# Gated linear attention and a rational MLP: the first super block half plain and half wide, the last one summed in natural order

## The chip, the core and the metric

The kernel runs on one core of one Trainium2 chip. The core has a matrix engine (TensorE, "PE" in the profile, with its weight loads shown apart as "PEld"), a vector engine (VectorE, "DVE"), a scalar engine (ScalarE, "ACT"), a general engine (GpSimd, "POOL") and a queue engine (SyncE, "SP") that here issues the DMA transfers. SBUF is the working memory of 128 partitions. PSUM is the memory of 8 banks into which TensorE writes its sums; one bank holds 512 float32 values in each partition.

The metric is the device time of one execution in microseconds. A run of a program gives one such time, and a profiled execution gives a trace beside it.

## The reference

```python
def _attn_ref(q, k, v, alpha):              # (4, 8, 768, 48) each
    state = zeros((B, H, D, D))
    for t in range(S):
        state = alpha[:, :, t, :, None] * state + einsum('bhd,bhe->bhde', k[:, :, t], v[:, :, t])
        y[:, :, t] = einsum('bhd,bhde->bhe', q[:, :, t], state)

def _moe_ref(x, w_in, w_out, a, b):         # x (3072, 384), w_in (384, 2048), w_out (2048, 384)
    h = x @ w_in
    P = a[0] + a[1]*h + a[2]*h**2 + a[3]*h**3
    Q = 1.0 + abs(b[0])*abs(h) + abs(b[1])*h**2
    return (P / (Q + 1e-06)) @ w_out
```

A gated linear attention over 4 batches of 768 tokens and 8 heads gives x with 384 columns; a two-layer MLP with a rational function between the layers follows. The weights arrive as float64, the rest as float32.

## The kernel before

**Attention.** The tokens are worked in 24 groups g of 128. For each group the kernel loads alpha, k and q (`load_akq`, four parts each, or `load_nat` for the first four groups), turns them so that channels lie on partitions (`turn_x`, L425, on VectorE, one transpose each for a, k and q; for the first four groups transposes on TensorE, L398, and copies, L417), takes running products of the gates (`suffix` L428, `prefix` L440, both scans on VectorE), scales k and q with them (L455, L458), multiplies scores (`sc_mm`, L472), masks them and adds up the output and the new state (`attn_mm`, L514 and L533). The scans read a small constant, the floor, from PSUM: groups below `G3` = 8 from bank 3, later ones from a cell in bank 5 that is written anew each time (`set_floor`, L344). The output of a group goes from PSUM to x (`x_hi` L556, `x_lo` L561).

**Weights.** `w_in` and `w_out` are loaded as 64-bit words in 16 blocks, ("i", j) and ("o", j) for j = 0 to 7 (`load_w`, L239 and L242). Each is made into float32 by integer steps: a scaled copy of the high word (`join_abs`, ScalarE, L249), a shift of the low word (`join_low`, VectorE, L255), the sign (`join_sign`, ScalarE L259 or VectorE L261) and the joining (`join`, VectorE, L274), which writes into the word buffer. For the wide jobs a block is brought back into a work buffer by a DMA (`bring`, L282) and split into a high and a low part (`split_hi` ScalarE L289, `split_lo` L294).

**MLP.** It is done in 96 jobs u. A job covers 512 values of h in each partition. The first 512 tokens (two segments of 256) take 16 "plain" jobs: float32 matmuls of unsplit weights, one block j (256 rows of h) and one segment at a time (`mlp_in` L589, `mlp_out_hi` L699). Their outputs lie in natural order, tokens on partitions, and are summed in banks 6 and 7 in two phases (`PHASES` = 0 and 6): first blocks 0 to 5 of both segments, then blocks 6 and 7, added onto the first part (`mlp_done`, L726 and L728) and stored (L731). The other 2560 tokens take 80 "wide" jobs, five super blocks m = 1 to 5 of 512 tokens with 16 jobs each, one for each 128 rows of h: nine float32r matmuls of split operands in (`wide_in`, L608), nine out (`wide_out`, L619), summed transposed, channels on partitions, in the three banks `O_BANKS` = 6, 7, 3. At the end of a super block VectorE turns the banks in 32x32 blocks into `parts` (`wide_done`, L625), and twelve scattered stores follow (`wide_store`, L629).

Between the two layers every job runs the rational function: ScalarE L635, L638, L644 (or GpSimd L642), L665, L668; GpSimd L647; VectorE L658, L662, L672, L675, L681. Wide jobs add the high part of the result (`act_gh`, ScalarE, L684) and the low part (`sub_gl`, GpSimd or now and then VectorE, L688).

**The end.** A check that all gates lie within limits (`guard`, `verdict_*`) gives one flag; all engines load it (L1049) and branch (L1050) past a general version of the kernel that isn't run with these inputs.

**The order.** All steps are registered with `add(key, engine, cost, function, arguments, what must come before, ..., alt=another engine)`. The order in which they are issued, and which engine takes a step with an alternative, is written out: the compressed list `ORDER` holds the number of each step, with a mark for the alternative. The costs and due times in `add` were for drawing up that list and have no effect when the kernel is built. Each engine works its own instructions strictly in this order.

Of the kernel before, what the change touches and what calls it, by code (L numbers as in the profile page):

```python
# [12 lines left out]
F32 = mybir.dt.float32  # L13
# [11 lines left out]
class Plan:  # L25
# [61 lines left out]
    'iiLEM!G^AxVZq1=s!@Cs<b-MI%3<!!JSYH~}S3M*mlpq@O8Cz;`V6#nB{yalH6QdkAkxfjpkFmA=mxHV7X$sxUm&fw*|',
# [35 lines left out]
    ';IEGteDD#2_aov5|GWtj1d)P7LE->{kN%TS7}x-V$iXKUC7^(VBtg_5X^<>P9z+Xb1Sx`)LChd}5GzO(qz=*qX@hh@`X',  # L123
    'EElCdd?I4l)L9gZ}}JD{Y|',
]


PACE, T0, LEAD = 5.0, 20.0, 2.0
NBI = 2
UPO = 16  # L130
NPH = 2
PHASES = (0, 6)
DMA = 0.49
SV = (1.1, 2.03, 0.67, 0.46)
IN = (1.09, 1.31)
OH = (0.722, 1.3)
WIDE = 0.229
G3 = 8
# [943 lines left out]
```

## Time and profile before

| | us |
|---|---|
| three runs | 549.97, 550.0, 548.46; median 549.97 |
| the profiled execution | 548.87, span of its trace 547.2 |
| TensorE busy | 522.2 (95%) |
| VectorE busy | 488.3 (89%) |
| ScalarE busy | 439.6 (80%) |
| GpSimd busy | 387.3 (71%) |
| DMA | 59.83 MB, mean 109 GB/s |
| granted TensorE clock | 0.991 of full |

The page of the profile gives busy time of each engine, a picture of the span in 40 slices, the chain of work that ended last, and the costliest groups of instructions by line, engine, output and input tile, with the number of instructions, busy time and mean duration of one, and the idle time before them. Matmuls overlap in the records, so the mean duration of one (397 ns in L608) is longer than their distance; the distance is read from the chain, where matmuls in a row are merged ("PE ps L608 x9"). A plain float32 matmul leaves two records, a float32r matmul one.

### The profile page before, as it was taken

What the parts mean: (1) busy time and instruction counts of PE and PEld (TensorE: products, weight loads), DVE (VectorE), ACT (ScalarE), POOL (GpSimd) and SP (SyncE); (2) the same over time, 40 slices, a digit from 0 to 9 for tenths busy, and PEclk for the clock granted to TensorE, in tenths of its full rate; (3) what the DMA queues carried; (4) which work ended last, traced back from release to release, by engine and by line L of the source; (5) the groups of instructions that cost most, each with busy time, mean ns of one, the idle gap of its engine ahead of it and who ended that gap; (6) DMA issues with size and microseconds to landing.
All of it is one profiled execution on the core that took longest, in us unless ns stands there. A gap on an engine that the chain in (4) does not pass through costs nothing.

```text
span 547.2 us, 11680 instructions
## 1 busy us (share of the span) xinstructions
PE 522.2 (95%) x4238; PEld 414.9 (76%) x4238; DVE 488.3 (89%) x753; ACT 439.6 (80%) x721; POOL 387.3 (71%) x358
## 2 busy tenths in 40 slices
PE   8879979999999999999999999999999999999990
PEld 8667657777778887788788787878888778878870
DVE  3999999999999998998999999999999897878871
ACT  3789869767889898888888978888878788889860
POOL 2557557778899898787877877867868576666750
PEclk9999999999999999999999999999999999999996
DMA  7898566556564543543366253523316120220003
GB/s 216 246 305 249 142 168 173 123 138 156 156 130 121 142 131 109 123 95 83 79 134 137 56 131 65 127 70 76 85 37 137 32 59 1 42 37 1 1 0 62
DMA packets 149343, 59.83 MB, mean 109 GB/s; under 512 B 133152, under 2 KB 141856, under 8 KB 149280
## 3 DMA queue, kind: packets, MB, share of 16 engines
q1 hardware_dynamic: 149280, 59.03, 43.6%
q8 instruction: 35, 0.57, 0.5%
q14 instruction: 28, 0.23, 0.1%
HBM read 47.98 MB, written 4.72 MB: 96 GB/s over the span
## 4 chain that ended last, share of the span: by engine, by line
PE 80%; DMA 6%; SPq 5%; DVE 4%; ACT 1%; issue 1%; DVEq 0%; ACTq 0%
PE ps L608 30%; PE ps L619 30%; PE ps L514 6%; PE ps L699 5%; PE ps L589 4%; PE ps L472 4%; DMA wo_words<-in_moe_w_out_dram 3%; DMA wi_words<-in_moe_w_in_dram 2%; SPq L374 2%; PE ps L490 1%; SPq L239 1%; PE ps L533 1%; SPq L381 1%; DMA raw_a<-in_alpha_dram 1%; SPq L210 1%
## 5 line engine op out<-in xcount | busy, mean ns | idle before, releaser
L608 PE MATMUL ps<-x,wi 128*128 128x512 f32 x720 | 195.0, 397 | 1.2 <-DVE t L681 1.2
L608 PEld LDWEIGHTS ps<-x,wi 128*128 128x128 f32 x720 | 133.9, 188 | 33.8 <-DVE t L681 2.4
L647 POOL TENSOR_TENSOR qm<-qm,ah 128x512 f32<-128x512 f32 x96 | 128.1, 1335 | 37.6 <-ACT qm L644 31.7
L619 PE MATMUL ps<-gh,wo 128*128 128x512 f32 x480 | 133.4, 398 | 0.0
L688 POOL TENSOR_TENSOR gl<-t,gh 128x512 fp32r<-128x512 f32 x70 | 91.0, 1302 | 39.1 <-ACT gh L684 19.4
L619 PEld LDWEIGHTS ps<-gh,wo 128*128 128x128 f32 x480 | 87.9, 188 | 20.4 <-ACT gh L684 0.3
L638 ACT ACTIVATE t<-ps,coef 128x512 f32<-128x512 f32 x96 | 74.1, 773 | 15.8 <-PE ps L608 9.3
L658 DVE TENSOR_TENSOR t<-t,ps 128x512 f32<-128x512 f32 x96 | 65.2, 679 | 19.1 <-ACT t L638 11.3
L665 ACT ACTIVATE ps<-qm,one_eps 128x512 f32<-128x512 f32 x96 | 66.3, 691 | 18.7 <-DVE t L662 12.4
L672 DVE SCALAR_TENSOR_TENSOR t<-t,coef,ps 128x512 f32<-128x512 f32 x96 | 70.7, 737 | 8.7 <-ACT ps L668 7.6
L635 ACT ACTIVATE ah<-ps 128x512 f32<-128x512 f32 x96 | 56.9, 592 | 25.1 <-PE ps L608 20.0
L662 DVE SCALAR_TENSOR_TENSOR t<-t,coef,ps 128x512 f32<-128x512 f32 x96 | 70.8, 738 | 1.3
L619 PE MATMUL ps<-gl,wo 128*128 128x512 f32 x240 | 69.1, 396 | 0.0
L681 DVE SCALAR_TENSOR_TENSOR t<-ps,t 128x512 f32<-128x512 f32 x96 | 65.8, 685 | 1.7
L675 DVE SCALAR_TENSOR_TENSOR ps<-qm,ps 128x512 f32<-128x512 f32 x96 | 65.9, 687 | 0.0
L642 POOL TENSOR_SCALAR qm<-ah,bab 128x512 f32<-128x512 f32 x44 | 37.8, 858 | 35.9 <-ACT ah L635 22.7
L668 ACT ACTIVATE ps<-ps 128x512 f32<-128x512 f32 x96 | 56.2, 586 | 1.8
L684 ACT ACTIVATE gh<-t 128x512 fp32r<-128x512 f32 x80 | 50.0, 625 | 5.1 <-DVE t L681 5.1
L619 PEld LDWEIGHTS ps<-gl,wo 128*128 128x128 f32 x240 | 44.3, 188 | 10.7 <-POOL gl L688 0.6
L589 PE MATMUL ps<-x,wi_words 128*128 128x256 f32 x192 | 47.3, 386 | 3.8 <-DVE t L681 3.4
L699 PE MATMUL ps<-wo_words,t 128*128 128x384 f32 x128 | 46.9, 490 | 0.0
L589 PEld LDWEIGHTS ps<-x,wi_words 128*128 128x128 f32 x192 | 35.3, 190 | 14.0 <-DVE t L681 4.5
(104 smaller groups left out, 748.2 us busy)
## 6 DMA issues: line engine op xcount, KB each, us to landing
raw_a<-in_alpha_dram SPq DMA_DIRECT2D x160, 48.0 KB, 2.1
raw_q<-in_q_dram SPq DMA_DIRECT2D x160, 48.0 KB, 2.1
raw_k<-in_k_dram SPq DMA_DIRECT2D x160, 48.0 KB, 2.1
wo_words<-in_moe_w_out_dram SPq DMA_DIRECT2D x8, 768.0 KB, 5.5
wi_words<-in_moe_w_in_dram SPq DMA_DIRECT2D x8, 768.0 KB, 6.7
tv<-in_v_dram SPq DMA_DIRECT2D x24, 192.0 KB, 3.4
wr<-in_alpha_dram SPq DMA_DIRECT2D x18, 256.0 KB, 3.0
out_dram<-parts SPq DMA_DIRECT2D x60, 64.0 KB, 2.5
```

Source lines behind the costliest of these rows:

```text
L589: nc.tensor.matmul(h, whole(("i", j))[:, kt * FU + ff, :], x[:, kt, 0, :], start=(kt == 0), stop=(kt == KT - 1),)
L608: nc.tensor.matmul(h_of(u), w(key)[:, kt * FU + f % FU, :], x[:, kt, xp, :], start=(n == 0), stop=(n == len(todo) - 1),)
L619: nc.tensor.matmul(bank(O_BANKS[dt]), w(("o", f // FU))[:, f % FU, dt * P : (dt + 1) * P], g, start=(f == 0 and first_w), stop=(f == NF - ...
L638: nc.scalar.activation(buf(s, "t1", u), h_of(u), AF.Identity, bias=a2, scale=a3)
L647: nc.gpsimd.tensor_tensor(buf(s, "qm", u), buf(s, "qm", u), buf(s, "ah", u), op=ALU.mult)
L662: nc.vector.scalar_tensor_tensor(t, t, a1, h_of(u), op0=ALU.add, op1=ALU.mult)
L665: nc.scalar.activation(h_of(u), buf(s, "qm", u), AF.Abs_reciprocal_sqrt, bias=one_eps)
L672: nc.vector.scalar_tensor_tensor(t, t, a0, h_of(u), op0=ALU.add, op1=ALU.mult)
L675: nc.vector.scalar_tensor_tensor(h_of(u), buf(s, "qm", u), 1.0 + 1e-6, h_of(u), op0=ALU.add, op1=ALU.mult)
L681: nc.vector.scalar_tensor_tensor(t, h_of(u), 2.0, t, op0=ALU.subtract, op1=ALU.mult, reverse0=True)
L688: eng.tensor_tensor(buf(s, "gl", u).rearrange("p a b -> p (a b)"), buf(s, "t1", u), gh, op=ALU.subtract)
L699: nc.tensor.matmul(o_of(tt), buf(s, "t1", u)[:, ff * SEG + tt * P : ff * SEG + (tt + 1) * P], whole(("o", j))[:, ff, :], start=(j == j0 an ...
```

## The change

- Of the first 512 tokens, the first half of h (blocks j = 0 to 3) is done in 8 plain jobs, and the second half in 8 wide ones (f = 8 to 15 of super block 0). `jobs` starts with 4 plain jobs of segment 0, then 4 of segment 1, then all wide jobs.
- Plain outputs are summed transposed (`plain_out`: six matmuls of 256 columns for four of 384), in the same three banks as wide ones, and super block 0 is evicted like the others. `mlp_done`, the two phases and the natural-order stores of the first tokens are gone.
- The first three plain jobs (`HALF`) multiply the two halves of their tokens apart (`plain_half`), the first half as soon as group 0 is there.
- x of super block 0 is kept whole in `x_whole`, in the space that later holds gh and gl, and split from there into high and low parts (`x_first_hi` ScalarE, `x_first_lo` GpSimd or VectorE).
- Weight blocks with j of 4 or more are joined in the work buffer and split from there; only blocks 0 to 3 are brought back by a DMA. Four work buffers are used throughout. The shift of the low word may run on GpSimd, as a multiplication and a minimum (10 of 16 do), and so may the scaled copy (2 of 16).
- k and q lie side by side and are turned by one VectorE instruction (`turn_qk`) for two.
- The floor cell in bank 5 is used from group 4 on (before: 8) and is written from a constant, 19 of 20 times on ScalarE.
- Super block 5, the last one, is summed in natural order in four banks (6, 7, 3, 4): four matmuls of 384 columns for three of 512 in `wide_out`. Two banks are evicted by VectorE and stored from SyncE's queue, two by ScalarE and stored from its own queue (`last_done`, `last_store`).
- `ORDER` is written anew. In it, compared with before: 82 gl steps on GpSimd for 70 and 6 on VectorE for 10; 17 q products on GpSimd for 23; 56 of the 96 steps of L642/L644 on GpSimd for 44.

```diff
-WIDE = 0.229
-G3 = 8
+WIDE = 0.232
+G3 = 4
+JP = 4
+HALF = 3
...
+    def kept(key):
+        return key[1] < JP
...
+    def join_low(eng, key):
+        w = word(key, 0)
+        if eng is nc.vector:
+            eng.tensor_scalar(w, w, 29, None, op0=ALU.logical_shift_right)
+        else:
+            eng.tensor_scalar(w, w, 2.0 ** -29, 7.0, op0=ALU.mult, op1=ALU.min)
...
         nc.vector.scalar_tensor_tensor(
-            o, wr[wr_slot(n)].rearrange("p (b n) -> p b n", n=w), 3,
+            o if kept(key) else hi_word, hi_word, 3,
...
+    def set_floor(eng, g):
+        if eng is nc.scalar:
+            eng.activation(floor_q, floor_s, AF.Copy)
+        else:
+            eng.tensor_copy(floor_q, floor_s)
...
+    def turn_qk(g):
+        x = raw_qk[0][:, 32 : 32 + 2 * LINE].rearrange("p (a t w) -> p a t w", a=4 * NPAIR, t=T4)
+        o = tqk[g % NQ].rearrange("p x a (n c t) -> p (x a n) t c", t=T4, n=2)
+        nc.vector.transpose(o, x[:, :, :, 0:32])
...
+    def x_first_hi(g):
+        cs = slice(g * C, (g + 1) * C)
+        nc.scalar.activation(x_of(0)[:, :, 0, cs], x_whole[:, :, cs], AF.Copy)
+
+    def x_first_lo(eng, g):
+        cs = slice(g * C, (g + 1) * C)
+        eng.tensor_tensor(
+            x_of(0)[:, :, 1, cs], x_whole[:, :, cs], x_of(0)[:, :, 0, cs].bitcast(F32), op=ALU.subtract
+        )
...
+    def plain_in(u, ff, c0, c1):
+        m, j = jobs[u][1:]
+        for kt in range(KT):
+            nc.tensor.matmul(
+                h_of(u)[:, ff * SEG + c0 : ff * SEG + c1], whole(("i", j))[:, kt * FU + ff, :],
+                x_whole[:, kt, m * SEG + c0 : m * SEG + c1],
+                start=(kt == 0), stop=(kt == KT - 1), skip_group_check=True,
+            )
+
+    def plain_half(u, part):
+        for ff in range(FU):
+            plain_in(u, ff, part * C, (part + 1) * C)
+
+    def plain_out(u, ff):
+        m, j = jobs[u][1:]
+        for dt in range(KT):
+            nc.tensor.matmul(
+                bank(O_BANKS[dt])[:, m * SEG : (m + 1) * SEG],
+                whole(("o", j))[:, ff, dt * P : (dt + 1) * P],
+                buf(fast_bufs, "t1", u)[:, ff * SEG : (ff + 1) * SEG],
+                start=(u == 0 and ff == 0), stop=False, skip_group_check=True,
+            )
...
     O_BANKS = (6, 7, 3)
+    T_BANKS = (6, 7, 3, SCB)
...
+        if m == NSUP - 1:
+            for tt in range(PER):
+                nc.tensor.matmul(
+                    bank(T_BANKS[tt], DM), g[:, tt * P : (tt + 1) * P], w(("o", f // FU))[:, f % FU, :],
+                    start=(f == 0 and first_w), stop=(f == NF - 1 and last_w),
+                )
+            return
...
+    def last_done(eng, tt):
+        o = parts[:, tt * DM : (tt + 1) * DM]
+        if eng is nc.scalar:
+            eng.activation(o, bank(T_BANKS[tt], DM), AF.Copy)
+        else:
+            eng.tensor_copy(o, bank(T_BANKS[tt], DM))
+
+    def last_store(eng, tt):
+        r = (NSUP - 1) * SUP + tt * P
+        eng.dma_start(out[r : r + P, :], parts[:, tt * DM : (tt + 1) * DM])
...
-    for j0, j1 in zip(PHASES, PHASES[1:] + (NU,)):
-        for m in range(NPH):
-            jobs += [(m, j, j0, j1 - 1) for j in range(j0, j1)]
+    jobs += [("plain", m, j) for m in range(2) for j in range(JP)]
     NUP = len(jobs)
-    jobs += [("wide", m, f) for m in range(1, NSUP) for f in range(NF)]
+    jobs += [("wide", m, f) for m in range(NSUP) for f in range(0 if m else FU * JP, NF)]
```

More of the change, by code (lines that the diff above doesn't have):

```diff
@@ L313, in tile_gla_then_rational_mlp @@
     tg = ring("tg", NTG, [P, NC4 * C1])
-    tk = ring("tk", NQ, [P, NC4, C])
-    tq = ring("tq", NQ, [P, NC4, C])
+    tqk = ring("tqk", NQ, [P, 2, NC4, C])
+    tq, tk = ([t[:, n] for t in tqk] for n in range(2))
     CB = 3 * BANK
@@ L570, in tile_gla_then_rational_mlp @@
         "ah": ring("ah", AB, [P, N]), "t1": ring("t1", TB, [P, N]), "qm": ring("qm", QB, [P, N]),
-        "gh": ring("gh", GB, [P, FU, SEG], F32R), "gl": ring("gl", GB - 1, [P, FU, SEG], F32R),
-        "part": [parts[:, i * DM : (i + 1) * DM] for i in range(2 * NPH)],
     }
-    outs = {}
     def buf(bufs, tag, u):
+        if tag not in bufs:
+            t = work.tile([P, 5 * BANK], F32R, tag="ghl", name="gh_gl")
+            t = [t[:, BANK * i : BANK * (i + 1)].rearrange("p (a b) -> p a b", b=SEG) for i in range(5)]
+            bufs["gh"], bufs["gl"] = t[0:GB], t[GB:]
         return bufs[tag][u % len(bufs[tag])]
@@ L580, in h_of, with mlp_in @@
         return bank(u % 3)
-    def mlp_in(u, ff, x=None):
-        m, j, _, _ = jobs[u]
+    def mlp_in(u, ff, x):
+        j = jobs[u][1]
         h = h_of(u)[:, ff * SEG : (ff + 1) * SEG]
-        plain = x is None and m < NBI
-        x = x_of(0)[:, :, :, m * SEG : (m + 1) * SEG] if x is None else x
         for kt in range(KT):
-            if plain:
-                nc.tensor.matmul(
-                    h, whole(("i", j))[:, kt * FU + ff, :], x[:, kt, 0, :],
-                    start=(kt == 0), stop=(kt == KT - 1),
-                )
-                continue
             for n, (w, xp) in enumerate(((hi, 0), (hi, 1), (lo, 0))):
@@ L695, in mlp_out_hi @@
     def mlp_out_hi(u, ff, s):
-        m, j, j0, j1 = jobs[u]
+        j = jobs[u][1]
         for tt in range(2):
-            if s is fast_bufs and u < UPO:
-                nc.tensor.matmul(
-                    o_of(tt), buf(s, "t1", u)[:, ff * SEG + tt * P : ff * SEG + (tt + 1) * P],
-                    whole(("o", j))[:, ff, :],
-                    start=(j == j0 and ff == 0), stop=(j == j1 and ff == FU - 1),
-                )
-                continue
             for w in (hi, lo):
@@ L708, in mlp_out_hi @@
                     w(("o", j))[:, ff, :],
-                    start=(j == j0 and ff == 0 and w is hi), stop=False,
+                    start=(j == 0 and ff == 0 and w is hi), stop=False,
                 )
     def mlp_out_lo(u, s):
-        m, j, j0, j1 = jobs[u]
+        j = jobs[u][1]
         for tt in range(2):
@@ L831, in general @@
                     )
-                jobs[:] = [(0, j, 0, NU - 1) for j in range(NU)]
+                jobs[:] = [(0, j) for j in range(NU)]
                 for u in range(NU):
@@ L951, in tile_gla_then_rational_mlp @@
             add(("xl", g), "DVE", 0.55, x_lo, (g,), [("xh", g)])
-    ends = {}
+        else:
+            add(("xr", g), "ACT", 0.5, x_first_hi, (g,), [("xh", g)])
+            add(("xl", g), "POOL", 1.0, x_first_lo, (g,), [("xr", g)], alt=("DVE", 0.55, True))
     fb = fast_bufs
```

304 lines of the change are left out of this document (153 added, 151 removed).

## The prediction

> **What bounds the kernel now.** I read the page first, then busy time by stretches, then the chain of waits.
>
> ```profile
> span 547.2 us, 11680 instructions
> PE 522.2 (95%) x4238; PEld 414.9 (76%) x4238; DVE 488.3 (89%) x753; ACT 439.6 (80%) x721; POOL 387.3 (71%) x358
> PE 80%; DMA 6%; SPq 5%; DVE 4%; ACT 1%; issue 1%; DVEq 0%; ACTq 0%
> ```
>
> An average over unlike stages says little. I cut the span where the chain of waits changes hands: at 78.88 (from there the chain is TensorE), at 134.36 (first wide matmuls, job 16) and at 534.15 (last output matmul). The columns are the stretch, its length and the busy time of each engine:
>
> ```profile
> core 0: us, PE busy (x) PEld busy (x) DVE busy (x) ACT busy (x) POOL busy (x), PEclk, DMA share, GB/s
> 0.00:78.88 78.88, 67.74 (x688) 54.34 (x688) 68.06 (x91) 60.51 (x81) 43.80 (x65) 1.00 0.77 219
> 78.88:134.36 55.48, 55.48 (x517) 41.17 (x518) 52.87 (x83) 42.96 (x61) 40.10 (x34) 1.00 0.59 154
> 134.36:534.15 399.79, 398.43 (x3032) 319.30 (x3031) 365.46 (x577) 336.18 (x579) 303.41 (x260) 1.00 0.36 83
> 534.15:547.20 13.05, 0.57 (x4) 0.10 (x3) 1.94 (x4) 0.00 (x0) 0.00 (x0) 0.62 0.39 65
> ```
>
> The reader is to see four stages with four limits. Start: VectorE. Its first scan begins only when alpha has been loaded, turned and copied:
>
> ```profile
> 1.00 0.48 DVE L340 MEMSET ps<- 128x512 f32 x1 [1.00 <-PEq L1066]
> ...
> 10.10 1.25 DVE L428 TENSOR_TENSOR_SCAN tg<-ta,ps 128x528 f32<-128x528 f32 x1 [6.41 <-ACT ta L417]
> ```
>
> so from then on it could work 68.78 us, and it worked 67.6 (68.06 less the 0.48 of set-up). Second stage: TensorE is full, but VectorE is full too, 52.87 of 55.48. Third: TensorE 99.7%, VectorE 91%. Tail: 13.05 us with no compute to speak of.
>
> **The change, part by part.**
>
> *TensorE, plain against wide.* In the chain, matmuls in a row show their true pitch:
>
> ```profile
> 80.44 1.29 PE ps L699 x4
> 81.73 1.29 PE ps L589 x6
> 471.74 2.06 PE ps L619 x9
> 473.80 2.06 PE ps L608 x9
> ```
>
> A plain job is two halves in and two out, 4 x 1.29 = 5.16 us. A wide one is 9 matmuls in and 9 out, 2 x 2.06 = 4.12. Plain jobs fall from 16 to 8, and 8 wide ones come: 8 x 1.04 = 8.3 us less. The transposed plain output costs the same: 12 records of 256 columns like L589, 2.58, for 8 of 384 like L699, 2.58. The first three jobs are cut into 128-column halves. The nearest row for short matmuls is 16 weight loads in a row with 128-column transposes:
>
> ```profile
> 6.07 1.75 PEld L398 LDWEIGHTS ps<-ident,raw_a 128*128 128x128 f32 x16
> ```
>
> 0.109 us each ((1.75 - 0.126) / 15, one load being 0.126 in its group), so 12 of them cost 1.31 against the 1.29 of a full half job. The upper end is that a short record costs what a full one does, 0.215: 2.58, six times +1.29, +7.7. I take 1.31, the nearer row; the six fall into stage one, where 67.74 busy us of 78.88 leave TensorE gaps, so 0 on the path. Without those gaps they cost 0.1 to 7.7.
>
> *VectorE up to job 16.* If VectorE is full, TensorE's 8.3 are only worth what VectorE lets through, so I counted VectorE's steps ahead of job 16's first matmul in both written orders. The prices:
>
> ```profile
> L255 DVE TENSOR_SCALAR wo_words<-wo_words 128x768 uint32<-128x768 uint32 x8 | 8.1, 1011 | 0.0
> L255 DVE TENSOR_SCALAR wi_words<-wi_words 128x768 uint32<-128x768 uint32 x8 | 6.7, 843 | 0.0
> L255 DVE TENSOR_SCALAR wo_words<-wo_words x8: 528/800/1639, 14.9 to 98.6; 128x768 uint32<-128x768 uint32 x8
> L261 DVE TENSOR_SCALAR wi_words<-wi_words 128x768 uint16<-128x768 uint16 x4 | 4.1, 1035 | 0.0
> L425 DVE STREAM_TRANSPOSE tk<-raw_k 128x512 f32<-128x512 f32 x20 | 14.1, 704 | 0.0
> L437 DVE RECIPROCAL ta<-tg 128x4 f32<-128x4 f32 x24 | 4.1, 171 | 0.2
> L458 DVE TENSOR_TENSOR tq<-tq,fp 128x512 f32<-128x512 f32 x1 | 1.2, 1232 | 0.0
> L455 DVE TENSOR_TENSOR tk<-tk,tg 128x512 f32<-128x512 f32 x1 | 0.9, 941 | 0.0
> L294 DVE TENSOR_TENSOR wi<-wr,wi 128x768 fp32r<-128x768 f32 x2 | 2.7, 1342 | 0.0
> L496 DVE TENSOR_TENSOR st_d<-st_s,tot 128x384 f32<-128x384 f32 x2 | 1.1, 550 | 0.0
> L681 DVE SCALAR_TENSOR_TENSOR t<-ps,t 128x512 f32<-128x512 f32 x96 | 65.8, 685 | 1.7
> ```
>
> Ten of 16 shifts (L255) go to GpSimd: -10 x 0.93 = -9.3, or -5.3 at the 0.53 of an undisturbed one. One sign step less: -1.0. Ten single transposes (5 of k, 5 of q) go, -7.0, and 5 double ones come: at most 2 x 0.70 = 1.40 each, +7.0; if one fixed part is saved, bounded by the 0.17 of the tiny reciprocal, +6.2. I take 7.0. Moved onto VectorE: three q products (+3.7), one k product (+0.9), two low parts of weights (+2.7), two decays (+1.1). Three elementwise steps more are already placed ahead: +2.1. Sum: +2.2 us, with ends +6.2 and +1.4. So VectorE needs 120.93 + 2.2 = 123.1 where it needed 120.93: the wide stage begins no earlier because TensorE has less to do.
>
> When does job 16 begin? The 9.6 us of idling ahead of the first scan stay (10.10 - 0.48): the same loads, turns and copies come first. With no other gap it begins at 132.7; with the other 3.8 of before (134.36 - 120.93 - 9.6) at 136.5. Three things let the gaps shrink: jobs 0 to 2 start on the first 128 tokens alone, eight of 16 weight blocks need no copy back through a DMA, and TensorE, 8 us less loaded, seldom keeps VectorE waiting. I take 133.6, a gain of 0.8.
>
> ScalarE does more there: six gh, six hi, four xr, each at most the 0.84 of
>
> ```profile
> L289 ACT ACTIVATE wi<-wr 128x768 fp32r<-128x768 f32 x8 | 6.7, 841 | 0.0
> L214 ACT ACTIVATE bab<-coef 128x2 f32<-128x2 f32 x1 | 0.2, 247 | 0.0
> ```
>
> so +13.4 on 103.5 of 134.36: off the path. GpSimd gains the most:
>
> ```profile
> L642 POOL TENSOR_SCALAR qm<-ah,bab 128x512 f32<-128x512 f32 x44 | 37.8, 858 | 35.9 <-ACT ah L635 22.7 <-DVE ps L675 5.5 <-DVE t L662 3.1
> L688 POOL TENSOR_TENSOR gl<-t,gh 128x512 fp32r<-128x512 f32 x70 | 91.0, 1302 | 39.1 <-ACT gh L684 19.4 <-PE ps L619 11.4 <-ACT ah L635 1.8
> ```
>
> A shift of 768 columns there is about 1.5 x 0.86 = 1.29; ten are 12.9, five gl 6.5, so from 83.9 us it goes to about 103 of 134. It is not the bound itself, but it stands in VectorE's way more often.
>
> L255 takes between 0.53 and 1.64 us for one and the same form. The Trainium skill (SBUF — State Buffer, Who interferes with whom) says that VectorE and GpSimd share a port pair as an exclusive lock held for a whole instruction, and the loser fully blocks; that spread agrees. By it a busier GpSimd stretches the joins and products that stay on VectorE, and the sum goes to the upper end of the ledger (a rival below) rather than to its middle.
>
> *Added waits.* From group 4 on (before: 8) a scan waits for a floor cell in bank 5, written after the state of two groups earlier, and ScalarE writes it now. Behind the waiting scan all of VectorE's queue stands. A write of one column costs about the 0.25 of L214; 20 of them exposed are +5 on VectorE, the upper end, and none the lower one. Sixteen fall behind job 16, where VectorE has 34 us of slack: I take 0. The first plain output now waits for the scans of groups 0 to 3, since it opens bank 3, where their floor lies:
>
> ```profile
> 24.20 1.22 DVE L440 TENSOR_TENSOR_SCAN fp<-ta,ps 128x528 f32<-128x528 f32 x1
> ...
> 42.84 1.56 PE L699 MATMUL ps<-wo_words,t 128*128 128x384 f32 x4
> ```
>
> The fourth pair of scans ended at 25.4, the first output ran at 42.8: 0. The first super block's eviction puts three VectorE transposes (1.9 us in the tail's row below) in place of four adds (2.2): 0. SyncE's queue gives out two more weight loads (768 KB each) and six more token loads (96 KB) ahead of job 8: 2.1 MB, some 10 us at 219 GB/s. The DMA engines stand free for 0.23 of 78.88, 18 us, so 0; without that cover up to 10, and the first wide jobs would wait for their weights.
>
> *Third stage.* The same 80 wide jobs, 399.79, except that the last 16 put out four matmuls of 384 columns for three of 512: 12 a job for 9. At 2.06 / 9 = 0.229 a matmul takes 512 columns; at 2.4 columns per ns (256 x 2 x 6 columns in 1.29 us) that is 0.213 and 0.016 fixed. 384 columns: 0.160 + 0.016 = 0.176, 12 x 0.176 = 2.11, +0.05 a job, +0.8 in all. If the pitch is bound by loading weights and stays 0.229: +0.69 a job, +11.0. Weight loads 0.109 apart (L398, some of them narrower) speak for the first. I take +0.8.
>
> *Tail.*
>
> ```profile
> 534.18 1.91 DVE L625 STREAM_TRANSPOSE parts<-ps 128x512 f32<-128x512 f32 x3 [2.74 <-PE ps L619]
> 534.92 7.29 SPq L629 DMA_DIRECT2D out_dram<-parts  x12
> 536.01 0.10 DVE L762 TENSOR_SCALAR ok<-ps 1x1 int32<-1x1 f32 x1
> L1050 PEldq COMPARE_BRANCH  x1: 4367/4367/4367, 536.8 to 536.8; - x1
> L1077 SPq EVENT_SEMAPHORE  x10: 17/28/28, 545.9 to 547.1; - x10
> L726 DVE TENSOR_TENSOR parts<-parts,ps 128x384 f32<-128x384 f32 x4 | 2.2, 550 | 0.2
> L728 ACT ACTIVATE parts<-ps 128x384 f32<-128x384 f32 x4 | 1.9, 487 | 0.0
> out_dram<-parts SPq DMA_DIRECT2D x4, 192.0 KB, 2.1
> ```
>
> Twelve scattered stores are issued for 7.29 us and land by 545.9. Now there are four evictions, two on VectorE (2 x 0.55) and two on ScalarE (2 x 0.49), and four plain-row stores, two on each queue: issued by about 2.0 us after the last matmul, landed 2.1 later, by 4.1. What is late next is TensorE's branch: it began 2.65 after the last matmul and took 4.37; with the verdict 0.75 earlier it is over at 6.3. Then the 1.3 us of the closing semaphores: 7.6 for 13.05, -5.4. Were the branch short, the stores would set 4.1 + 1.3 = 5.4, -7.6; were it 2 us longer, -3.4. The Trainium skill (Runtime: NRT & Kernel Launch, Instruction fetch mechanics) says that a taken branch outside the fetched window waits for a DMA fetch of its page; that fits the 4.37, and by it the branch stays whatever the stores do.
>
> Sum against the profiled span of 547.2: -0.8 + 0.8 - 5.4 = -5.4. The profiled execution took 548.87, the median is 549.97, and the two lie in one spread of 1.5; from them come 543.5 and 544.6, and I say 544.0.
>
> **The rivals.**
>
> *TensorE sets the early pace.* VectorE's 0.93 shifts and 1.23 products are mostly blocking; if the new order avoids that, all of the 8.3 comes through and job 16 begins at 126. For it: TensorE is at 55.48 of 55.48 in stage two. Against it: VectorE is at 95% there. 544.0 - 7.5 = 536.5.
>
> *Weight loading binds the last 16 jobs.* 12 x 0.229 each, from the first output of the last super block on, where TensorE is full. 544.0 + 10.2 = 554.2, slower. It decides as soon as the pitch at 384 columns is over 0.20 (16 x 12 x 0.029 = 5.6).
>
> *GpSimd and VectorE block each other more.* The upper end of the ledger, +6.2, with the 4.0 of gaps: 140.6, so 544.0 + 7 = 551.
>
> *The tail does not shorten*, because the branch or the stores of two queues take as long as before: 544.0 + 5.4 = 549.4.
>
> **How the numbers follow.** Forecast 0.54, early TensorE 0.21, weight loading 0.07, blocking 0.12, tail 0.06. The forecast's own range is 540 to 547.5; to it comes the early-TensorE case below and part of blocking and tail above: 536.5 to 550. What a measurement can tell from no change is about 0.3%, 1.6 us. Faster: 0.54 + 0.21 and the near halves of tail and blocking, 0.79. Same: 0.10. Slower: weight loading and the far half of blocking, 0.11.
>
> **What would show it.** Job 16's first wide matmuls near 133.6 with VectorE over 93% busy up to there; 12 output matmuls of 384 columns in 2.1 us; 7 to 8 us from the last matmul to the end; TensorE full between. It is wrong if the wide stage begins before 130 or after 138, or if the last 16 jobs stretch.

## The result and the profile after

The changed kernel takes 556.81 us (median of four runs, 556.58 to 557.96), the kernel before 549.99 on the same chip: a ratio of 1.0134, interval 1.0111 to 1.0157. It is slower by 7 us where 6 us less were forecast. The profiled execution took 556.58, span 554.9.

The page of the changed kernel: span, busy time, GpSimd in 40 slices, and the chain that ended last.

```profile
span 554.9 us, 11838 instructions
PE 525.1 (95%) x4338; PEld 433.3 (78%) x4338; DVE 483.8 (87%) x716; ACT 435.9 (79%) x737; POOL 434.1 (78%) x382
...
POOL 4559999998999888778867868798857857766782
...
PE 77%; POOL 10%; DMA 3%; SPq 3%; ACT 2%; DVE 2%; issue 1%; ACTq 0%; DVEq 0%; POOLq 0%
```

GpSimd had no place in the chain before; now it has 10%. It gained 46.8 us of work (387.3 to 434.1), VectorE lost 4.5. GpSimd's slices in the kernel before were these, lighter above all in slices 4 to 9 (of 13.7 us each):

```profile
POOL 2557557778899898787877877867868576666750
```

Busy time in the four stages, cut as in the prediction: at 78.88, at the first wide matmul of job 16, which now comes at 145.85 (134.36 before), and near the last output matmul (columns as there: stretch, length, then busy TensorE, weight loads, VectorE, ScalarE, GpSimd, then TensorE's granted clock, the DMA engines' share and GB/s). The 145.85, like every later start of job 16 in this text, is the start of the matmul's own record. The 134.36 is a start in the chain of waits; the record before begins at 133.91, so starts before and after compare to within half a microsecond.

```profile
0.00:78.88 78.88, 67.72 (x766) 59.13 (x770) 61.04 (x86) 58.09 (x80) 55.74 (x67) 0.96 0.88 230
78.88:145.85 66.97, 56.61 (x492) 45.62 (x484) 56.15 (x78) 53.10 (x82) 63.22 (x42) 0.92 0.43 97
145.85:546.00 400.15, 400.15 (x3086) 328.26 (x3085) 365.58 (x550) 323.76 (x576) 315.12 (x275) 1.00 0.36 78
546.00:554.90 8.90, 0.65 (x6) 0.29 (x4) 1.07 (x3) 0.98 (x2) 0.00 (x0) 0.71 0.30 98
```

In the second stage GpSimd is at 63.22 of 66.97 (94%), and TensorE, which was full there, is idle for 10.4. The chain of waits gives the last output matmul exactly:

```profile
535.80 0.69 PE ps L656 x3
536.49 10.05 PE ps L669 x56
```

It ends at 546.54. So the start is 11.5 us longer (145.85 - 134.36; 11.9 by the two records), the third stage 400.69 for 399.79 (+0.9), the tail 8.36 for 13.05 (-4.7). The sum is +7.7, the difference of the spans. The whole loss stands ahead of job 16.

What GpSimd does there is shown by its groups (mean ns of one after the bar), the shifts and the scaled copies of the weights:

```profile
L264 POOL TENSOR_SCALAR wo_words<-wo_words 128x768 uint32<-128x768 uint32 x5 | 16.1, 3223 | 0.4
L264 POOL TENSOR_SCALAR wi_words<-wi_words 128x768 uint32<-128x768 uint32 x5 | 15.4, 3076 | 6.3 <-DMA wi_words<-in_moe_w_in_dram 6.0
...
L254 POOL TENSOR_SCALAR wr<-wi_words 128x768 f32<-128x768 f32 x1 | 2.2, 2198 | 0.0
L254 POOL TENSOR_SCALAR parts<-wi_words 128x768 f32<-128x768 f32 x1 | 2.2, 2169 | 0.0
```

Ten shifts take 31.5 us, 3.15 each, where the prediction priced 1.29 and 12.9. The chain of waits of the changed kernel, here from 80.96 us to 91, is that queue:

```profile
80.96 3.56 POOL wo_words L264
84.52 0.08 issue
84.60 1.27 POOL tqk L476
85.87 0.76 POOL qm L709
86.63 0.08 issue
86.71 2.91 POOL wi_words L264
89.62 0.07 issue
89.69 1.27 POOL qm L714
```

Between two shifts GpSimd does what other engines wait for: the k products (L476), the polynomial of a job (L709, L714). Each stands behind a shift of 3 us. TensorE's timeline shows what that costs (in brackets its idle time and the releaser):

```profile
94.92 1.65 PE L656 MATMUL ps<-x,wi 128*128 128x512 f32 x3 [6.88 <-POOL wi L304]
...
118.30 1.23 PE L493 MATMUL ps<-tqk 48*128 48x128 f32 x16 [3.24 <-POOL tqk L476]
```

These two waits, for a low part of weights and for a k product, are 10.1 of TensorE's 10.4 idle us of the second stage. TensorE is also slower behind them: its granted clock is 0.92 in this stage (1.00 before), and six records of one and the same kind take 2.76 us behind the first wait and 1.46 later (why the clock is lower was not tried):

```profile
96.37 2.76 PE L642 MATMUL ps<-t,wo_words 128*128 128x256 f32 x6
...
110.20 1.46 PE L642 MATMUL ps<-t,wo_words 128*128 128x256 f32 x6
```

### The profile page after: what moved, and what is told of

Its sections match the earlier page's. It is cut to its first block, busy times and chain, and to the rows that moved or that the text cites. A ratio compares the mean times of both kernels' runs of the same rounds, so it can differ in the third digit from the quotient of the medians.

```text
span 554.9 us, 11838 instructions
## 1 busy us (share of the span) xinstructions
PE 525.1 (95%) x4338; PEld 433.3 (78%) x4338; DVE 483.8 (87%) x716; ACT 435.9 (79%) x737; POOL 434.1 (78%) x382
## 4 chain that ended last, share of the span: by engine, by line
PE 77%; POOL 10%; DMA 3%; SPq 3%; ACT 2%; DVE 2%; issue 1%; ACTq 0%; DVEq 0%; POOLq 0%
PE ps L656 32%; PE ps L675 28%; PE ps L669 6%; PE ps L535 5%; PE ps L493 4%; POOL wi_words L264 2%; DMA wi_words<-in_moe_w_in_dram 2%; POOL wo_words L264 2%; POOL qm L714 2%; PE ps L511 1%; DMA wo_words<-in_moe_w_out_dram 1%; SPq L397 1%; PE ps L554 1%; POOL tqk L476 1%; POOL qm L709 1%
## 5 line engine op out<-in xcount | busy, mean ns | idle before, releaser
L656 PE MATMUL ps<-x,wi 128*128 128x512 f32 x792 | 215.5, 399 | 7.1 <-POOL wi L304 6.9
L675 PE MATMUL ps<-gh_gl,wo 128*128 128x512 f32 x648 | 182.9, 403 | 0.0
L714 POOL TENSOR_TENSOR qm<-qm,ah 128x512 f32<-128x512 f32 x96 | 127.2, 1326 | 28.7 <-ACT qm L711 20.4
L675 PEld LDWEIGHTS ps<-gh_gl,wo 128*128 128x128 f32 x648 | 119.8, 190 | 28.4 <-issue 0.4
L755 POOL TENSOR_TENSOR gh_gl<-t,gh_gl 128x512 fp32r<-128x512 f32 x82 | 106.3, 1297 | 24.2 <-ACT gh_gl L751 12.4
L702 ACT ACTIVATE ah<-ps 128x512 f32<-128x512 f32 x96 | 57.0, 593 | 29.5 <-PE ps L656 25.0
L732 ACT ACTIVATE ps<-qm,one_eps 128x512 f32<-128x512 f32 x96 | 66.3, 690 | 17.1 <-POOL qm L714 13.7
L709 POOL TENSOR_SCALAR qm<-ah,bab 128x512 f32<-128x512 f32 x56 | 45.2, 808 | 31.9 <-ACT ah L702 22.6
L751 ACT ACTIVATE gh_gl<-t 128x512 fp32r<-128x512 f32 x88 | 55.1, 627 | 5.0 <-DVE t L748 5.0
L669 PE MATMUL ps<-wo,gh_gl 128*128 128x384 f32 x192 | 38.0, 339 | 0.0
L449 DVE TENSOR_TENSOR_SCAN tg<-ta,ps 128x528 f32<-128x528 f32 x24 | 29.8, 1243 | 9.2 <-ACT ta L433 8.9
L669 PEld LDWEIGHTS ps<-wo,gh_gl 128*128 128x128 f32 x192 | 34.4, 188 | 2.3 <-ACT gh_gl L751 0.2
L504 POOL TENSOR_SCALAR_AFFINE_SELECT sc<-sc 128x1024 f32<-128x1024 f32 x24 | 27.4, 1144 | 10.2 <-ACT sc L500 9.8
L493 PEld LDWEIGHTS ps<-tqk 48*128 48x128 f32 x384 | 23.7, 187 | 13.5 <-issue 5.8
```

The source lines that it names most:

```text
L656: nc.tensor.matmul(h_of(u), w(key)[:, kt * FU + f % FU, :], x[:, kt, xp, :], start=(n == 0), stop=(n == len(todo) - 1),)
L669: nc.tensor.matmul(bank(T_BANKS[tt], DM), g[:, tt * P : (tt + 1) * P], w(("o", f // FU))[:, f % FU, :], start=(f == 0 and first_w), stop=( ...
L675: nc.tensor.matmul(bank(O_BANKS[dt]), w(("o", f // FU))[:, f % FU, dt * P : (dt + 1) * P], g, start=(f == 0 and first_w), stop=(f == NF - ...
L714: nc.gpsimd.tensor_tensor(buf(s, "qm", u), buf(s, "qm", u), buf(s, "ah", u), op=ALU.mult)
L732: nc.scalar.activation(h_of(u), buf(s, "qm", u), AF.Abs_reciprocal_sqrt, bias=one_eps)
L755: eng.tensor_tensor(buf(s, "gl", u).rearrange("p a b -> p (a b)"), buf(s, "t1", u), gh, op=ALU.subtract)
```

## The experiments

Where a run compares starts, the number is mostly the start of ScalarE's absolute value of job 16 (`act_ah`, L635 before, L702 changed), one of the two ScalarE steps that read its wide matmuls' sums. The expectations call it the gate activation, and below it is "the activation": 138.46 before, 149.87 changed. It comes from one profiled execution of each kernel, and runs of one kernel differ by 1.4 to 6 us in time, so differences of a microsecond in it are not read.

### The ten shifts on VectorE, and on GpSimd in the kernel before

```diff
 # changed kernel, in Plan
+        self.other -= {k for k in self.other if k[0] == "low"}
```

> The changed kernel with its ten GpSimd shifts of weight words (L264, 31.5 us of GpSimd in its trace) back on VectorE, at the same places of the written order. Theory A, GpSimd's in-order queue is filled by these shifts and holds everything behind them: job 16 begins near 136 instead of 145.85 (VectorE takes over: 9.6 us ahead of the first scan, some 126 us of work), and the time is 546 to 549, faster than before. Rival B, the wide second half of super block 0 itself (splitting x and weights, gh and gl, the floor from group 4) is what is late: job 16 stays past 143 and the time past 553.

```diff
 # kernel before; ON_POOL: the ten blocks that the changed kernel shifts on GpSimd
+        w = word(key, 0)
+        if key in ON_POOL:
+            nc.gpsimd.tensor_scalar(w, w, 2.0 ** -29, 7.0, op0=ALU.mult, op1=ALU.min)
+        else:
+            nc.vector.tensor_scalar(w, w, 29, None, op0=ALU.logical_shift_right)
```

> The kernel before, with only the same ten shifts (the same weight blocks) done on GpSimd, as the change does them. Theory A: GpSimd goes from 43.8 of the first 78.88 us to over 70, its queue holds the masks and products behind the shifts, job 16 begins 4 to 12 us later than 134.36, and the time is 553 to 561. Rival B: VectorE is 9.3 us lighter and the start no later, the time is 545 to 550.

With the shifts back on VectorE the changed kernel takes 550.63 (ratio to before 1.003, 1.0003 to 1.0058): some 6 of the 7 us are gone. With the shifts on GpSimd the kernel before takes 552.21 (1.0068, 1.0041 to 1.0096), although VectorE is relieved of ten of them. So the shift's place costs time in both orders. In the kernel before with the shifts on GpSimd, job 16 begins at 138.93, 5.0 later than at 133.91, within theory A's 4 to 12; the time stays under theory A's 553 to 561, and GpSimd is busy for 57.38 of the first 78.88 us, not for over 70. The changed kernel with the shifts on VectorE misses theory A's 546 to 549 from above, and its activation of job 16 comes at 142.03, 3.6 later than before. The stages of this second kernel:

```profile
0.00:78.88 78.88, 67.06 (x806) 59.60 (x807) 65.38 (x93) 60.52 (x83) 41.57 (x63) 0.96 0.86 231
78.88:138.02 59.14, 54.45 (x446) 43.29 (x444) 57.62 (x82) 50.89 (x78) 46.26 (x35) 0.97 0.49 109
```

Now VectorE is at 57.62 of 59.14, and GpSimd at 46.26. Job 16's first matmul is at 138.02. The queue that binds has moved from GpSimd to VectorE.

### The shifts left out

```diff
 # changed kernel, join_low
+        if eng is nc.gpsimd:
+            return
```

> The changed kernel without the ten shifts by 16 bits that it gave to GpSimd: no engine does them, so the low parts of ten weight blocks are wrong words, and the output is not the reference's; every other instruction stays where the change put it. Theory A (the prediction's ledger is right but for the price of the shift on GpSimd, 3.15 us and not 1.29): with 31.5 us out of GpSimd's queue the first wide matmul of the second iteration begins near the forecast 133.6, the gate activation of job 16 near 137.7 (changed kernel 149.87, before 138.46), and the time is about 545 (556.6 - 12). Rival B (the wide jobs' other work on VectorE sets the late start, as the 3.6 us suggest that stayed when VectorE took the shifts back): the activation stays at 141 or later and the time at 549 or more.

(The shift is by 29 bits, not by the 16 that the expectation names.) 540.84 (0.9833, 0.9814 to 0.9851), activation of job 16 at 133.37: theory A, and 4 us past it, as the shifts are gone altogether, also the 12.9 us that the forecast had given them. The stages:

```profile
0.00:78.88 78.88, 70.16 (x821) 62.15 (x822) 64.36 (x93) 64.44 (x88) 42.40 (x66) 0.98 0.87 231
78.88:129.36 50.48, 48.60 (x430) 39.20 (x429) 49.09 (x72) 47.08 (x74) 43.14 (x33) 1.00 0.58 127
```

Job 16 begins at 129.36, 16.5 us earlier than with the shifts on GpSimd and 8.7 earlier than with them on VectorE. VectorE's busy time up to job 16 differs by 9.6 between those last two (123.0 and 113.45): what is put on VectorE there passes almost whole into the start.

### VectorE relieved in another way

```diff
 # changed kernel, in Plan
+        self.other -= {k for k in self.other if k[0] in ("low", "abs") or (k[0] in ("q", "k", "d", "tot") and k[1] < 8)}
+        self.other |= {k for k in keys if k[0] == "lo"}
```

> The changed kernel with the ten shifts back on VectorE, the two scaled copies of the weights (2.2 us each on GpSimd) back on ScalarE, and in their place the normalised q, the normalised k, the decay and the totals of the first super block's groups and the three low parts of the projections moved from VectorE to GpSimd: about 9.9 us less on VectorE, 6 more on GpSimd net of the copies. Theory A (with the shifts on VectorE it is VectorE that is full up to job 16 and sets the remaining 3.6 us): the activation of job 16 comes at 135 to 138 (142.03 with the shifts back alone), the time is 544 to 547. Rival B (GpSimd's queue order, or the longer path of q and k through GpSimd, sets it): no gain, or later than 142 and 550 or more.

```diff
 # changed kernel, in Plan
+        self.other -= {k for k in self.other if k[0] in ("low", "abs")}
```

> The changed kernel with the ten shifts back on VectorE and only the two scaled copies (2.2 us each) moved from GpSimd back to ScalarE. If VectorE alone sets the remaining 3.6 us: as with the shifts back alone, 550.6, activation of job 16 at 142 within 0.5. If GpSimd's queue still holds part of it: 546 to 549, activation 139 to 141.

The first takes 549.5 (1.0002, 0.9975 to 1.003), activation at 141.13. Theory A's numbers did not come; the interval overlaps that of the run with the shifts alone on VectorE, so rival B's "no gain" stands. The edit also did less than expected: VectorE's busy time up to job 16 fell by 5.0 (123.0 to 118.0), not by 9.9, and GpSimd's rose by 12.6, not by 6. The first job's activation comes at 36.06 for 33.28 with the shifts alone on VectorE, so 2.8 us are lost ahead of job 0 (the products of the first groups are among the steps moved; that they are the cause was not tried); from job 0 to job 16 it takes 105.1 for 108.8. So the stretch in which VectorE is full became shorter and the one ahead of it longer; which of the moved steps did either was not tried. The second takes 550.67 (1.0022, 0.9997 to 1.0046), the same time as with the shifts alone moved back, as the first of its two expectations had it. Its profiled execution has the activation at 144.66, later than either expectation; that execution is one of the slower ones of its kernel (551.59 of 549.33 to 552.27), and the point stays open.

### The tail alone, on and off

```diff
 # kernel before
+        if m == NSUP - 1:
+            for tt in range(PER):
+                nc.tensor.matmul(bank(T_BANKS[tt], DM), g[:, tt * P : (tt + 1) * P], w(("o", f // FU))[:, f % FU, :], ...)
+            return
 # and the evictions and stores of the last super block as in the changed kernel
```

> The kernel before, with only the last 512 tokens summed in natural order in four banks and stored from two queues. The trace of the changed kernel has 8.9 us from its last output matmul to the end where before has 13.05, and its stage of wide jobs is 0.4 longer: so 546.2, 3.8 less. If the shorter tail hung on something else of the change, 549 to 550. If the 384-column matmuls cost TensorE 0.229 each after all, 556 or more.

```diff
 # changed kernel: the last super block summed transposed, as the others
-        if m == NSUP - 1:
+        if False:
 # and last_done, last_store call wide_done, wide_store of that super block
```

> The changed kernel with the last super block summed and stored as before (three banks, VectorE transposes, twelve scattered stores). If the tail is worth what the two traces say, 3.8 more: 560.6 against 556.8. If the natural order costs TensorE more than it saves at the end, 557 or less.

544.8 (0.9919, 0.9899 to 0.994) and 563.11 (1.0274, 1.0225 to 1.0324). Alone, this part is worth 4.8 us (549.56 before on that chip), and without it the changed kernel loses 6.3 by the medians, 7.7 by the two ratios. In the kernel before it does what was forecast for it (+0.8 and -5.4), and job 16 begins within 0.9 us of where it does without the edit, at 134.56 and at 146.70. Both runs give more than the 3.8 that was expected of them. In the second the tail is 14.8 us (561.3 - 546.51), 1.7 longer than in the kernel before, which is why this part weighs more there.

### Why the shift takes 3 us

```diff
 # kernel before, behind its end; w0, w1 contiguous, pair and pairf every second word of a buffer
+    for _ in range(2):
+        nc.gpsimd.tensor_scalar(w0, w1, 0.5, None, op0=ALU.mult)                          # L1051
+        nc.gpsimd.tensor_scalar(w0, pairf[:, :, 1], 0.5, None, op0=ALU.mult)              # L1052
+        nc.gpsimd.tensor_scalar(w0, pairf[:, :, 1], 0.5, 7.0, op0=ALU.mult, op1=ALU.min)  # L1053
+        nc.gpsimd.tensor_scalar(pairf[:, :, 0], pairf[:, :, 0], 0.5, 7.0, op0=ALU.mult, op1=ALU.min) # L1054
+        nc.gpsimd.tensor_scalar(wr[0], wr[1], 2.0 ** -29, 7.0, op0=ALU.mult, op1=ALU.min) # L1055
+        nc.gpsimd.tensor_scalar(pair[:, :, 0], pair[:, :, 0], 2.0 ** -29, 7.0, op0=ALU.mult, op1=ALU.min) # L1056
+        nc.vector.tensor_scalar(pair[:, :, 0], pair[:, :, 0], 29, None, op0=ALU.logical_shift_right)      # L1057
```

> The kernel before with single instructions of 768 elements per partition added behind its end, two of each kind, to read durations alone; its time is longer by them. On GpSimd: contiguous float32 with one operation, float32 with a stride of two words with one and with two operations, the same in place, contiguous uint32 with the shift's two operations, and the shift itself (stride two, in place); on VectorE the shift. Theory A (the integer type makes the 3.15 us): contiguous uint32 is near 3 us and strided float32 near 1.3. Rival B (the stride makes it): strided float32 is near 2 to 3 us and contiguous uint32 near 1.3. Rival C (the second operation makes it): two-operation forms are twice the one-operation form whatever the type.

GpSimd's groups in the last stretch of that kernel:

```profile
L1054 POOL TENSOR_SCALAR parts<-parts 128x768 f32<-128x768 f32 x2 | 5.7, 2837 | 4.1 <-SPq L1060 4.0
L1056 POOL TENSOR_SCALAR parts<-parts 128x768 uint32<-128x768 uint32 x2 | 5.7, 2836 | 0.2
L1055 POOL TENSOR_SCALAR wr<-wr 128x768 uint32<-128x768 uint32 x2 | 5.5, 2772 | 0.2
L1053 POOL TENSOR_SCALAR wr<-parts 128x768 f32<-128x768 f32 x1 | 2.8, 2808 | 0.1
L1051 POOL TENSOR_SCALAR wr<-wr 128x768 f32<-128x768 f32 x1 | 2.5, 2506 | 0.1
L1052 POOL TENSOR_SCALAR wr<-parts 128x768 f32<-128x768 f32 x1 | 2.2, 2160 | 0.1
```

Neither theory A nor B: words of integer type and a stride of two change the time by less than 0.1 us between the forms with two operations (L1054 and L1056 differ in the type alone: 2837 and 2836 ns). The shift takes 2.84 with nothing else running, so at most 0.3 of its 3.15 comes from other engines. Nor is it rival C in its size, since one operation is little cheaper than two. What stays is that every form here takes 1.7 to 2.2 times the 1.29 that the polynomial's row had led to, so the next run took that row's form apart:

```diff
 # kernel before, behind its end; bab holds two scalars for each partition
+        nc.gpsimd.tensor_scalar(w0[:, :512], w1[:, :512], bab[:, 1:2], bab[:, 0:1], op0=ALU.mult, op1=ALU.add) # L1052
+        nc.gpsimd.tensor_scalar(w0[:, :512], w1[:, :512], 0.5, 7.0, op0=ALU.mult, op1=ALU.add)                 # L1053
+        nc.gpsimd.tensor_scalar(w0[:, :512], w1[:, :512], 0.5, 7.0, op0=ALU.mult, op1=ALU.min)                 # L1054
+        nc.gpsimd.tensor_scalar(w0, w1, bab[:, 1:2], bab[:, 0:1], op0=ALU.mult, op1=ALU.add)                   # L1055
+        nc.gpsimd.tensor_scalar(w0, w1, 0.5, 7.0, op0=ALU.mult, op1=ALU.add)                                   # L1056
+        nc.gpsimd.tensor_scalar(w0, w1, bab[:, 1:2], bab[:, 0:1], op0=ALU.mult, op1=ALU.min)                   # L1057
+        nc.gpsimd.tensor_scalar(w0, pairf[:, :, 1], bab[:, 1:2], bab[:, 0:1], op0=ALU.mult, op1=ALU.add)       # L1058
+        nc.gpsimd.tensor_scalar(pair[:, :, 0], pair[:, :, 0], bab[:, 1:2], bab[:, 0:1], op0=ALU.mult, op1=ALU.min) # L1059
```

> The kernel before with single GpSimd instructions added behind its end, two of each kind, to read durations alone; its time is longer by them. They take the steps apart from the row that priced the shift (512 contiguous float32, two operations, scalars from a tile: 0.78 to 0.86 us) to the shift itself (768 words with a stride of two, in place, two operations, immediate scalars: 2.84 us where nothing else runs). Theory A (scalars that stand in the instruction are what is slow): 512 elements with immediate scalars take 1.5 to 2 us, 768 with scalars from a tile about 1.2, and the strided uint32 form with scalars from a tile 1.2 to 2. Rival B (the length: something changes between 512 and 768): 512 with immediate scalars takes 0.8 to 0.9, 768 with scalars from a tile 2.5 or more. Rival C (the operation min in place of add is slow): only the forms with min are above 1.3.

```profile
L1059 POOL TENSOR_SCALAR parts<-parts,bab 128x768 uint32<-128x768 uint32 x2 | 6.0, 2985 | 2.3 <-SPq L1062 2.3
L1057 POOL TENSOR_SCALAR wr<-wr,bab 128x768 f32<-128x768 f32 x2 | 5.8, 2922 | 0.2
L1054 POOL TENSOR_SCALAR wr<-wr 128x512 f32<-128x512 f32 x2 | 3.8, 1918 | 0.2
...
L1058 POOL TENSOR_SCALAR wr<-parts,bab 128x768 f32<-128x768 f32 x2 | 2.0, 1018 | 0.2
L1055 POOL TENSOR_SCALAR wr<-wr,bab 128x768 f32<-128x768 f32 x2 | 2.0, 982 | 0.2
L1056 POOL TENSOR_SCALAR wr<-wr 128x768 f32<-128x768 f32 x2 | 1.7, 831 | 0.2
L1052 POOL TENSOR_SCALAR wr<-wr,bab 128x512 f32<-128x512 f32 x2 | 1.5, 769 | 0.0
L1053 POOL TENSOR_SCALAR wr<-wr 128x512 f32<-128x512 f32 x2 | 1.2, 618 | 0.2
```

Rival C of this run, and clearly: the three forms with a minimum take 1.9 to 3.0 us, the five with an addition 0.6 to 1.0. With the addition, scalars from a tile cost 0.15, a stride 0.04. From 512 to 768 columns the addition grows by 0.21 (0.83 ns a column), the minimum by 0.85 (2772 of the run before - 1918 here, over 256: 3.3 ns a column). The multiplication alone of the run before (2.16 to 2.51) belongs with the slow forms. So it is not the minimum that is slow among quick forms: of those measured, the multiplication with an addition is the one quick pair.

### The shift written with an addition

```diff
 # changed kernel, join_low on GpSimd
-            eng.tensor_scalar(w, w, 2.0 ** -29, 7.0, op0=ALU.mult, op1=ALU.min)
+            eng.tensor_scalar(w, w, 2.0 ** -29 * (1 - 2.0 ** -10), 7.5 * 2.0 ** -10 - 0.5, op0=ALU.mult, op1=ALU.add)
```

> The changed kernel, whole, with one operation of the ten GpSimd shifts replaced: a multiplication and an addition (times 2^-29 less a thousandth, minus nearly a half, rounded to the nearest: the same three bits but for a word in some hundreds) where a multiplication and a minimum stood. Theory A (the late start is the price of the operation pair on GpSimd, 2.8 us with the minimum against 0.83 with the addition, 768 elements, each where nothing else ran): the shift takes 1.0 to 1.3 us, ten about 12, the 12.9 of the prediction; the gate activation of job 16 comes between 133.4 (shifts left out) and 137.7 (the forecast), and the time is 541 to 545. Rival B (words of integer type are slow on GpSimd whatever the operations): the shift stays near 2.8 to 3.2, the time at 556. Rival C (the shift becomes cheap, and its place in GpSimd's order still holds the gates): the activation later than 140, the time above 547.

542.16 (0.9874, 0.9824 to 0.9923): theory A. The groups and the stages of this kernel:

```profile
L264 POOL TENSOR_SCALAR wo_words<-wo_words 128x768 uint32<-128x768 uint32 x5 | 5.8, 1170 | 0.4
L264 POOL TENSOR_SCALAR wi_words<-wi_words 128x768 uint32<-128x768 uint32 x5 | 4.5, 910 | 6.4 <-DMA wi_words<-in_moe_w_in_dram 6.1
```

```profile
0.00:78.88 78.88, 70.48 (x821) 62.66 (x822) 63.90 (x93) 64.04 (x87) 49.98 (x73) 0.98 0.87 232
78.88:132.80 53.92, 50.47 (x431) 40.33 (x429) 50.80 (x72) 47.54 (x74) 47.39 (x36) 0.97 0.53 118
```

Ten shifts take 10.3 us, and job 16 begins at 132.80, 13 us earlier than in the changed kernel; the activation comes at 136.81. The order of all steps is the same in both, so the price of this one form is the cause. Of the 13 us, 3.4 are TensorE's busy time for the same matmuls (67.72 + 56.61 = 124.3 up to job 16 in the changed kernel, 70.48 + 50.47 = 121.0 here), which goes with the lower granted clock behind the waits; the rest is idle time. In the queue of GpSimd the same stretch now reads:

```profile
73.21 0.96 POOL L264 TENSOR_SCALAR wo_words<-wo_words 128x768 uint32<-128x768 uint32 x1
74.25 1.87 POOL L476 TENSOR_TENSOR tqk<-tqk,tg 128x512 f32<-128x512 f32 x1
76.11 1.47 POOL L709 TENSOR_SCALAR qm<-ah,bab 128x512 f32<-128x512 f32 x1
77.66 0.91 POOL L264 TENSOR_SCALAR wi_words<-wi_words 128x768 uint32<-128x768 uint32 x1
```

The first of these shifts began at 80.96 in the changed kernel. Two further steps in this direction:

```diff
 # as above, and the scaled copies on GpSimd
-            eng.tensor_scalar(o, x, 2.0 ** -112, None, op0=ALU.mult)
+            eng.tensor_scalar(o, x, 2.0 ** -112, 0.0, op0=ALU.mult, op1=ALU.add)
```

> As the run before, and the two scaled copies on GpSimd (2.2 us each, a multiplication alone) also written as a multiplication and an addition of zero. If GpSimd's queue still holds the start: 1 to 2.4 us faster than the run before. If VectorE or TensorE holds it: the same within 0.5.

```diff
 # as above, and in Plan
+        self.other |= {k for k in keys if k[0] == "low"}
```

> As the run before, and all 16 shifts on GpSimd: the six that the changed kernel left on VectorE (0.55 us each, 3.3) go there too, for about 7 us. If VectorE's sum sets the start: 2 to 3 us faster than the run before, 539 to 542. If GpSimd's queue does, or the first blocks' path through it: the same or slower.

541.74 (0.9885, 0.982 to 0.9951) and 540.08 (0.9852, 0.9804 to 0.99). The copies fall from 2.2 to 0.93 us, and the time stays within the spread, the second of the two expectations. With all 16 shifts on GpSimd the median is 1.7 below the run before it, near what was expected if VectorE's sum sets the start, but the intervals overlap, so the order of these three is not shown. Each of them is faster than both kernels of the case.

## Why the prediction was wrong

**The step that failed is the price of the shift on GpSimd**, "about 1.5 x 0.86 = 1.29; ten are 12.9". It was taken from the polynomial's row (L642), an instruction of the same name and engine with a multiplication and an addition. The shift has a multiplication and a minimum, and measured 3.15, ten 31.5. I scaled the row by its columns and gave the price no upper end, though the trace had no row with the shift's operations on GpSimd. The nearest row of 768 columns there, the subtraction of L294 at 1.85, would have raised it, but not to 3.15. From it came "It is not the bound itself", and this fell too: GpSimd was busy for 63.22 of 66.97 in the second stage, and the products, polynomials and low parts of weights that stood behind the shifts came late. Job 16 began at 145.85 where 133.6 was forecast and 138 named as the point from which the forecast is wrong.

**With the price that the prediction had assumed, its sum comes out.** The kernel with the addition has job 16 at 132.80 (-1.6, or -1.1 by the two records; forecast -0.8). Its last output matmul ends at 533.50:

```profile
523.47 10.03 PE ps L669 x56
```

so its third stage takes 400.70 (+0.9; forecast +0.8), and its tail 541.7 - 533.50 = 8.2 (-4.9; forecast -5.4). Together -5.5 against the forecast's -5.4, and 542.16 for 544.0. The tail alone is worth 4.8 in the kernel before, so all the rest of the change brings some 2 us with the cheap shift, and the two intervals overlap.

**The ledger of VectorE was wrong twice**, and that the start still comes out is luck. Its items as listed add up to +0.2, not +2.2 (with ends of +4.2 and -0.6), so it should have said 121.1 us up to job 16 and not 123.1. And it was too large: in the kernel with the addition VectorE is busy for 63.90 + 50.80 = 114.7 and idle for 18.1, where about 10.5 of idling were forecast. Less work and more idling cancelled. The shifts saved more than 9.3, since the six that stay take 0.57 each (3.4 in all, for 14.8 of the 16 before); the double turn measured 1.24, near its lower end of 1.23; and q products cost 0.69 each on VectorE where 1.23 was taken. So "if VectorE is full, TensorE's 8.3 are only worth what VectorE lets through" is supported, since 9.6 us more on VectorE made job 16 8.7 later, but VectorE is not the only engine that holds the start.

**The rivals.** *TensorE sets the early pace* did not come: no run brought job 16 to 126; the earliest, without the shifts, is 129.36, and with all 16 shifts as additions on GpSimd it is

```profile
129.66 1.32 PE L657 MATMUL ps<-x,wi 128*128 128x512 f32 x5
```

*Weight loading binds the last 16 jobs* fell: 56 matmuls of 384 columns in 10.05 us are 0.179 each, 2.15 a job, against 0.176 and 2.11 forecast and 0.229 for the rival. *GpSimd and VectorE block each other more* had the right place and sign, and 551 for 556.8 (549 with the ledger added up as above), but the wrong cause: it needed a lock between the two engines, and the shift takes 2.84 of its 3.15 alone. The waits it built on are in the trace before: the VectorE shift at 58.01 takes 1.64, starts inside a GpSimd product (57.26 to 59.23) and ends 0.4 behind it. In the changed kernel none of the six that stay on VectorE is stretched: they take 0.51 to 0.58. The joins that stay on VectorE (L284) do take longer in the changed kernel, 20.6 us in all against 17.2 in the kernel with the addition. That fits the rule of the Trainium skill (SBUF — State Buffer, Who interferes with whom) which the prediction had weighed, but no run separates it from the rest, and 3.4 us are not 13. *The tail does not shorten* fell.

**The tail was mis-sized by 0.8**, 8.36 for 7.6. What the changed kernel's stores and branch show (durations in us for the landing, in ns for the branch):

```profile
DMA to landing us min/median/max: 2.3/3.4/4.7
...
L1110 PEldq COMPARE_BRANCH  x1: 4727/4727/4727, 547.7 to 547.7; - x1
L1110 SPq EVENT_SEMAPHORE  x8: 17/17/17, 553.0 to 553.5; - x8
L1137 SPq EVENT_SEMAPHORE  x10: 17/28/28, 553.6 to 554.8; - x10
```

The branch on TensorE is late next, as forecast: it begins 1.2 after the last matmul (forecast 1.9), takes 4.73 (4.37) and ends at 552.4. But four stores of 192 KB at once land in up to 4.7 us, not 2.1, so the last one is there about when the branch ends. From the branch's end to the end of the span it is 2.5 where 1.3 was taken: the closing steps (L1137, from 553.6) do take 1.3, and the 1.2 us ahead of them, with eight steps of SyncE from 553.0, had no term. Which of the two, stores or branch, sets the end here was not tried. The branch's 4.7 us again fit what the Trainium skill (Runtime: NRT & Kernel Launch, Instruction fetch mechanics) says of a taken branch that leaves the fetched window.

## What to carry to other kernels

Price a moved instruction by a row with the same operations, not only the same engine, name and shape; where no row has them, its upper bound is open, and that belongs in the range. Before work is given to an engine that looks free on average, look at what stands behind it in that engine's queue in that very stage, and how long a single instruction holds the queue. When a change of many parts loses, undoing one part and leaving one part out locate the loss; rewriting one instruction then shows whether the rest was right.

## What the runs showed of the hardware

- On GpSimd a tensor-scalar instruction with a multiplication and an addition takes 0.83 us for 128x768 float32 (0.98 with scalars from a tile), one with a multiplication and a minimum 2.8 to 2.9, one with a multiplication alone 2.2 to 2.5; a multiplication by 2^-112 fell from 2.2 to 0.93 in the kernel when an addition of zero was appended.
- Type and stride hardly matter there: uint32 with a stride of two, in place, took 2.84 with the minimum and 0.91 to 1.17 with the addition. The same shift on VectorE takes 0.56.
- One VectorE transpose of 128x1024 takes 1.24 us, two of 128x512 1.40.
- A float32r matmul of 384 columns follows its neighbour after 0.179 us, one of 512 after 0.229.
- The same VectorE shift took 0.53 to 1.64 us in the kernel before; the one at 58.01 ended 0.4 us behind a GpSimd product that had begun before it.
- Shortly after 6.9 us without a matmul, six plain matmul records of 256 columns took 2.76 us, and 1.46 later; the granted clock of that stage was 0.92.
